# A fused attention and mixing kernel: V loaded by single transfers, first halves of keys and queries fetched first, and GpSimd bounding early weight pieces

## Chip, cores and metric

The kernel runs on one core of a Trainium2 chip. The metric is the device time of one execution in microseconds (us), lower is better. The core has a matrix engine (TensorE, PE in the rows; PEld is its weight load), VectorE (DVE), ScalarE (ACT), GpSimd (POOL), and SyncE (SP), which here only issues DMA transfers. SPq, ACTq and POOLq are the queues on which these engines issue them.

## The reference, cut to what matters

```python
def phi(x):                                   # random-feature map, 128 features
    h = einsum('bhsd,md->bhsm', x * D**-0.25, omega) - |x|^2 / 2
    return exp(h - max(h)) / sqrt(m)
q_p, k_p = phi(q), phi(k)                     # 8 batches, 8 heads, 576 rows, D = 64
kv  = einsum('bhsm,bhsd->bhmd', k_p, v);  z = sum(k_p, rows)
x   = (q_p @ kv) / (q_p @ z + 1e-6)           # [8, 576, 512] after joining the heads
u   = x + (x^T @ U @ V)^T                     # mixing over the 576 rows, rank 32
out = u + relu(u @ w_ch1) @ w_ch2             # 512 -> 2048 -> 512
```

The arrays U, V, w_ch1 and w_ch2 arrive as 64-bit floats and are turned into 32-bit floats inside the kernel.

## The kernel before

**Attention** goes over 16 units (a pair of batches by two heads each way). A round has nine steps (`for s in range(NR * NT + 7)`): round r handles the keys of one unit and the queries of an earlier one, two parts with 128 rows of 2 batches by 2 heads in each step. Round 0 handles the keys of two units. One step is a chain: the raw tile (`kt` for the first part, `qt` for the second) is transposed by VectorE, 384 columns for three steps at once (`turn`, L643); ScalarE rounds it to `xh` (L647); GpSimd takes the rest `xl` (L651); TensorE projects with `omh` and `oml` (`project`, L771 to L773) into `p_p`; VectorE takes the negated maximum `nm` (`peak`, L779); ScalarE the exponential `e` (L786); TensorE uses `e` for keys (`p_kv`) or turns it for queries (`p_q`), which ScalarE and VectorE copy to `eT` (L714) for `p_n`. Two values split one 32-bit product into three fast ones.

**Loads** of keys and queries: a raw tile has 1152 columns, of which `load(0)` brings the first 576 and `load(1)` the others, four transfers of 72 KB each (`blocks`, L616 to L626). The first group of three steps (columns 0 to 383) needs `load(0)` alone, the second (384 to 767) both. Nearly all transfers are issued by SyncE, one after the other, in an order that a list scheduler makes from the program order. The values are loaded by `load_values` (L665, L670).

**Pieces of weights** are decoded beside attention, one slot every second or third step (`decoding`, L125). The first piece is U, the next two are the halves of V (`v_jobs`, L375), then come pieces of w_ch1. For a piece, ScalarE takes the magnitude (L141) and the low word (L144), and then VectorE has three instructions: the bounds (L159, a maximum and a minimum), a shift (L160), and the sign (L163); GpSimd adds the low word (L184). `fine` is 13 in attention, the number of the pieces that are decoded this way there and just behind it. V is replicated four times over the partitions, so each half is loaded by four transfers (L381 to L385).

**Mixing** of a pair of batches (`mixing`, L418) is interleaved with the attention of the next; at the end of attention the last one overlaps with the first products of the feed-forward part. That part is done in seven-product form (`unit`, L987) with 4 column groups of w_ch1 and chunks of 512 rows, then the second matrix. The tables `BEGIN` and `PACE`, and the lists of engines in `prepare(..., lows=..., sums=...)`, are written out by hand; they say at which product a piece of helper work is emitted and on which engine it is.

## Time and profile before

| quantity | value |
|---|---|
| median of 3 runs | 1039.98 us (1036.77 to 1040.38) |
| the profiled execution's own time | 1022.2 us |
| span of the profiled execution | 1020.3 us, 23875 instructions |
| TensorE busy | 1002.5 us (98%) |
| VectorE busy | 844.5 us (83%) |
| ScalarE busy | 614.6 us (60%) |
| GpSimd busy | 516.2 us (51%) |
| mean granted TensorE clock | 0.997 of full speed |

The span runs from the first to the last instruction of the program, the execution's own time lies 1.9 us over it, and the runs without a profile are longer than both. Busy shares are means over stages with different limits: attention up to about 300 us, a transition to about 330 us, then the two matrix products of the feed-forward part.

### The profile page before, as it was taken

The page shows a single profiled execution, that of the slowest core. Times are in us where ns is not written, and L with a number is a line of the kernel's source. Part 1 is how long each engine was busy: PE and PEld are TensorE (multiplying, and loading weights), DVE is VectorE, ACT ScalarE, POOL GpSimd, SP SyncE. Part 2 cuts the span into 40 slices and gives each one's busy share as a digit, 9 for nine tenths or more (in the row PEclk, how much of TensorE's full clock was granted, in tenths as well). Part 3 has the DMA queues.
Part 4 walks back from the last instruction along what each step waited for, and adds up shares of the span by engine and source line. Part 5 has one row for each costly group of instructions (what it writes and reads, how often), then busy time and mean ns, then how long its engine had stood idle before and what let it go on. Part 6 is the DMA issues. An engine that isn't in the chain of part 4 may idle for free.

```text
span 1020.3 us, 23875 instructions
## 1 busy us (share of the span) xinstructions
PE 1002.5 (98%) x8497; PEld 980.9 (96%) x8497; DVE 844.5 (83%) x1507; ACT 614.6 (60%) x1483; POOL 516.2 (51%) x453
## 2 busy tenths in 40 slices
PE   8999999999999999999999999999999999999998
PEld 7899999999997999999999999999999999999998
DVE  4699898898899796766567565779999999999995
ACT  5889989989885557446355354665444454454442
POOL 4446966867536353323415314525756646646543
PEclk9899999999999999999999999999999999999999
DMA  7688588587444785888679768874555455455451
GB/s 141 137 164 157 115 197 161 112 188 145 88 105 113 214 202 144 225 243 207 179 204 238 183 178 273 258 234 155 176 169 204 146 176 177 145 176 176 145 177 51
DMA packets 380518, 175.51 MB, mean 172 GB/s; under 512 B 275552, under 2 KB 353376, under 8 KB 375920
## 3 DMA queue, kind: packets, MB, share of 16 engines
q1 hardware_dynamic: 378000, 173.67, 64.3%
q8 instruction: 67, 1.10, 0.5%
q10 hardware_dynamic: 2368, 0.30, 0.2%
q14 instruction: 51, 0.42, 0.1%
q0 software_dynamic: 32, 0.03, 0.0%
HBM read 109.97 MB, written 63.96 MB: 170 GB/s over the span
## 4 chain that ended last, share of the span: by engine, by line
PE 58%; DMA 1%; DVE 0%; issue 0%; ACT 0%; DVEq 0%
PE p_q L1409 10%; PE p_p L1409 10%; PE p_n L1409 7%; PE p_n L1028 7%; PE p_p L1028 5%; PE p_q L1028 5%; PE p_kv L1409 5%; PE p_kv L1028 4%; PE p_m L1028 3%; PE p_m L1409 2%; DMA raw<-in_moe_w_ch_dram 1%; DVE g L1014 0%; DMA g<-g 0%; ACT g L1010 0%; DVE u L1334 0%
## 5 line engine op out<-in xcount | busy, mean ns | idle before, releaser
L786 ACT ACTIVATE e<-p_p,nm 128x128 f32<-128x128 f32 x576 | 166.4, 397 | 24.9 <-DVE nm L779 15.9
L1247 ACT CAST gh<-gs 128x512 fp32r<-128x512 f32 x140 | 86.8, 623 | 150.4 <-DVE gs L1219 82.9
L1219 POOL TENSOR_TENSOR gs<-graw 128x512 f32<-128x512 f32 x66 | 108.5, 1654 | 125.2 <-DMA graw<-g 72.0
L1010 ACT ACTIVATE g<-g 128x512 f32<-128x512 f32 x105 | 66.4, 634 | 148.0 <-DVE g L1014 91.7
L651 POOL TENSOR_TENSOR xl<-xT,xh 128x384 fp32r<-128x384 f32 x96 | 97.5, 1033 | 99.9 <-ACT xh L647 82.8
L1254 DVE TENSOR_TENSOR gl<-gs,gh 128x512 fp32r<-128x512 f32 x140 | 132.9, 955 | 7.7 <-ACT gh L1247 6.8
L779 DVE TENSOR_REDUCE nm<-p_p 128x4 f32<-128x512 f32 x144 | 98.1, 683 | 27.4 <-ACT e L786 10.3
L184 POOL TENSOR_TENSOR wf<-wf,low 128x512 int32<-128x512 int32 (+2 forms) x35 | 44.0, 1257 | 130.0 <-ACT g L1010 71.8
L771 PE MATMUL p_p<-omh,xh 128*128 128x256 f32 x288 | 93.2, 324 | 1.9 <-ACT e L786 1.6
L1334 POOL TENSOR_TENSOR u<-u,p 128x256 f32<-128x256 f32 x72 | 80.9, 1153 | 24.8 <-DVE u L1334 22.4
L1254 DVE TENSOR_TENSOR gl<-graw,gh 128x512 fp32r<-128x512 f32 x107 | 83.1, 800 | 3.1 <-ACT gh L1247 3.1
L772 PE MATMUL p_p<-oml,xh 128*128 128x256 f32 x288 | 81.5, 283 | 0.0
L773 PE MATMUL p_p<-omh,xl 128*128 128x256 f32 x288 | 81.4, 283 | 0.0
L1409 PE MATMUL p_p<-wh,gh 128*128 128x256 f32 x288 | 79.5, 276 | 0.0
L1409 PE MATMUL p_p<-wl,gh 128*128 128x256 f32 x288 | 79.5, 276 | 0.0
L1409 PE MATMUL p_p<-wh,gl 128*128 128x256 f32 x288 | 79.5, 276 | 0.0
L1247 ACT CAST gh<-graw 128x512 fp32r<-128x512 f32 x107 | 63.7, 621 | 25.6 <-PE p_n L1409 4.9
L1409 PE MATMUL p_q<-wh,gl 128*128 128x256 f32 x276 | 76.3, 276 | 0.0
L1409 PE MATMUL p_q<-wh,gh 128*128 128x256 f32 x276 | 76.2, 276 | 0.0
L1409 PE MATMUL p_q<-wl,gh 128*128 128x256 f32 x276 | 76.2, 276 | 0.0
L729 PE MATMUL p_n<-kv,eT 128*128 128x65 f32 x512 | 73.2, 272 | 2.9 <-ACT eT L714 1.9
L729 PEld LDWEIGHTS p_n<-kv,eT 128*128 128x128 f32 x512 | 68.3, 194 | 6.2 <-ACT eT L714 2.4
(291 smaller groups left out, 3935.8 us busy)
## 6 DMA issues: line engine op xcount, KB each, us to landing
g<-g SPq DMA_DIRECT2D x282, 128.0 KB, 2.6
graw<-g SPq DMA_DIRECT2D x35, 1024.0 KB, 5.2
raw<-in_moe_w_ch_dram SPq DMA_DIRECT2D x23, 512.0 KB, 4.7
u_dram<-ut SPq DMA_DIRECT2D x36, 256.0 KB, 2.5
u<-u_dram SPq DMA_DIRECT2D x36, 256.0 KB, 2.6
out_dram<-u SPq DMA_DIRECT2D x36, 256.0 KB, 2.5
kt<-in_k_dram SPq DMA_DIRECT2D x120, 72.0 KB, 2.5
qt<-in_q_dram SPq DMA_DIRECT2D x120, 72.0 KB, 2.5
```

The source lines that it names most:

```text
L651: nc.gpsimd.tensor_tensor(out=self.xl[-1], in0=self.turned, in1=f32(self.xh[-1]), op=ALU.subtract)
L729: nc.tensor.matmul(pn[:, h, :], eT[:, h, :], kv[:, h, s // 5, :], start=True, stop=True)
L771: nc.tensor.matmul(o, part.xh[g][:, ts], oh, start=True, stop=False)
L772: nc.tensor.matmul(o, part.xh[g][:, ts], ol, start=False, stop=False)
L773: nc.tensor.matmul(o, part.xl[g][:, ts], oh, start=False, stop=True)
L779: nc.vector.tensor_reduce(out=self.nm[:, :n], in_=self.pp[:, :n], axis=AX.X, op=ALU.max, negate=True)
L786: nc.scalar.activation(out=self.e[:, j, :], in_=self.pp[:, j, :], func=AF.Exp, bias=self.nm[:, j : j + 1])
L1028: K(nc.tensor.matmul(p[:, f, :], x[:, k, fs], y[:, k, :], start=first, stop=(k == 1 and y is ul), skip_group_check=True,))
L1219: K(engine.tensor_tensor(out=to, in0=self.val[x], in1=self.val[y], op=op))
L1247: K(nc.scalar.copy(out=h, in_=v))
L1254: K(nc.vector.tensor_tensor(out=l, in0=v, in1=f32(h), op=ALU.subtract))
L1409: K(nc.tensor.matmul(acc[bank][:, half, :], x[:, ks], y[:, f, :], start=(now.s == 0 and k == 0 and half == 0 and x is h and y is wh), stop ...
```

## The change

Each half of V is loaded by one transfer with a repeated source instead of four. Omega is loaded on ScalarE's queue instead of GpSimd's, ahead of the four transfers of the second unit's first half, and the table load of ScalarE comes behind them. The halves `omh` are copied by VectorE instead of ScalarE. From the second round on, first halves are issued first: keys `load(0)`, queries `load(0)`, keys `load(1)`, queries `load(1)`, instead of both halves of the keys first. In step 3 the second part's transpose is placed behind the maximum. For pieces below 13, the bounds are applied by GpSimd right behind the magnitude, and VectorE's first slot is left empty. In the feed-forward part some helper operations change engines and some are emitted a product earlier or later.

```diff
+        bounded = fine if fine < 99 else 0
...
                 K(nc.scalar.activation(out=mags[i], in_=f32(raws[i][:, :, 1]), func=AF.Abs))
+                if i < bounded:
+                    nc.gpsimd.tensor_scalar(mags[i], mags[i], _MOST, _LEAST, ALU.min, ALU.max)
...
+            if i < bounded:
+                slots[0] = None
...
             def load(raw):
-                for j in range(4):
-                    nc.sync.dma_start(
-                        out=raw[j * R : (j + 1) * R].rearrange("r s w -> r (s w)"),
-                        in_=words(V)[:, 2 * c : 2 * c + S],
-                    )
+                rows = words(V)[:, 2 * c : 2 * c + S]
+                nc.sync.dma_start(
+                    out=raw.rearrange("p s w -> p (s w)"), in_=rows.unsqueeze(0).broadcast_to([4, R, S])
+                )
...
-                rest = nc.vector if last and t not in (0, 1, 2, 3, 4, 5, 6, 7) else nc.gpsimd
+                rest = nc.vector if last and t not in (1, 2, 3, 4, 5, 6, 7) else nc.gpsimd
...
-    nc.gpsimd.dma_start(out=once, in_=omega)
+    nc.scalar.dma_start(out=once, in_=omega)
+    keys[0].load(0)
+    keys[1].load(0, 4)
+    for p in keys:
+        p.load(1)
     nc.vector.memset(warm, 0.0)
     K(nc.scalar.activation(out=warm, in_=warm, func=AF.Exp))
-    keys[0].load(0)
-    keys[1].load(0, nc.scalar)
-    for p in keys:
-        p.load(1)
...
-        nc.scalar.copy(out=omh[r, j, :], in_=pom[r])
+        nc.vector.tensor_copy(out=omh[r, j, :], in_=pom[r])
...
                 new[0].load(0)
-                if r:
-                    new[0].load(1)
             if t == 1:
                 new.append(Queries(r + last, 1))
                 new[1].load(0)
                 if r == 0:
                     for p in keys[:2]:
                         p.load_values(1, "t")
-                    new[0].load(1)
+                new[0].load(1)
                 new[1].load(1)
...
-    BEGIN = (3, 5, 6, 9, 11, 13, 14, 16, 17, 18, 19)
+    BEGIN = (3, 5, 6, 8, 11, 13, 14, 16, 17, 18, 19)
...
-    PACE = {2: (0, 1, 1, 0, 1, 2, 1), 3: (3, 3, 3, 3, 5, 3, 0), 4: (2, 1, 2, 1, 2, 4, 2), 5: (1, 1, 2, 1, 1, 1, 2)}
+    PACE = {2: (0, 1, 1, 0, 1, 2, 1), 3: (3, 3, 4, 3, 5, 3, 0), 4: (1, 1, 2, 1, 2, 4, 2), 5: (2, 1, 1, 1, 1, 1, 2)}
```

On SyncE, these rows stand behind the load of U; they run to the values of the fourth unit's keys. `kt` and `qt` are the tiles of the third round (round 2), `x` the values of its keys. Before:

```order
L382 DMA raw<-in_moe_V_dram 32x576 x4
L665 DMA x<-in_v_dram 128x4x64 x2
L670 DMA x<-in_v_dram 64x2x64
L665 DMA x<-in_v_dram 128x4x64 x2
L670 DMA x<-in_v_dram 64x2x64
L623 DMA kt<-in_k_dram 32x18x32 x8
L623 DMA qt<-in_q_dram 32x18x32 x8
L382 DMA raw<-in_moe_V_dram 32x576 x4
L665 DMA vt_134<-in_v_dram 128x4x64 x2
```

And of the change:

```order
L387 DMA raw<-in_moe_V_dram 128x1x576
L669 DMA x<-in_v_dram 128x4x64 x2
L674 DMA x<-in_v_dram 64x2x64
L669 DMA x<-in_v_dram 128x4x64 x2
L674 DMA x<-in_v_dram 64x2x64
L627 DMA kt<-in_k_dram 32x18x32 x4
L627 DMA qt<-in_q_dram 32x18x32 x4
L627 DMA kt<-in_k_dram 32x18x32 x4
L627 DMA qt<-in_q_dram 32x18x32 x4
L387 DMA raw<-in_moe_V_dram 128x1x576
```

The first half of the queries now has seven transfers fewer ahead of it behind U: three of V and four of the keys.

On VectorE, at the first transposes of round 2 (`xT<-kt`, `xT<-qt`), with the maxima `nm` of two of the steps before it. Before:

```order
L643 STREAM_TRANSPOSE xT<-kt 128x384
L714 COPY eT<-p_q 128x256
L779 TENSOR_REDUCE nm<-p_p 128x4
L160 TENSOR_SCALAR wf<-wf 128x288
L739 TENSOR_SCALAR rec<-p_n 128x4
L643 STREAM_TRANSPOSE xT<-qt 128x384
L740 RECIPROCAL rec<-rec 128x4
```

And of the change:

```order
L647 STREAM_TRANSPOSE xT<-kt 128x384
L647 STREAM_TRANSPOSE xT<-qt 128x384
L718 COPY eT<-p_q 128x256
L783 TENSOR_REDUCE nm<-p_p 128x4
L163 TENSOR_SCALAR wf<-wf 128x288
L743 TENSOR_SCALAR rec<-p_n 128x4
```

The transpose of the queries has moved ahead of a copy `eT` and a maximum.

## Rows read from the trace of the kernel before

**Rows 1.** Busy us (x instructions) of each engine by stage: stretch, length, engines, clock, DMA.

```profile
40.00:60.00 20.00, 18.09 (x134) 17.44 (x133) 14.91 (x37) 13.53 (x47) 6.69 (x8) 0.83 0.72 131
60.00:300.00 240.00, 235.89 (x1954) 224.84 (x1952) 214.95 (x531) 215.13 (x695) 158.88 (x160) 1.00 0.69 145
100.00:120.00 20.00, 19.75 (x158) 18.57 (x156) 17.27 (x39) 19.13 (x61) 20.00 (x21) 1.00 0.75 141
300.00:330.00 30.00, 27.71 (x200) 24.31 (x199) 28.25 (x60) 19.59 (x49) 19.78 (x15) 1.00 0.52 104
330.00:480.00 150.00, 147.71 (x1254) 145.72 (x1253) 111.27 (x182) 80.98 (x156) 54.05 (x47) 1.00 0.78 205
480.00:1000.00 520.00, 519.97 (x4577) 519.70 (x4577) 443.26 (x632) 253.87 (x446) 254.31 (x184) 1.00 0.61 188
```

**Rows 2.** The same view, 38 to 52 us; order: PE, PEld, DVE, ACT, POOL, clock.

```profile
38.00:40.00 2.00, 2.00 (x20) 2.00 (x19) 0.98 (x3) 1.81 (x8) 0.92 (x1) 1.00 0.62 100
...
42.00:44.00 2.00, 0.77 (x8) 0.63 (x6) 1.86 (x7) 0.79 (x3) 0.66 (x1) 1.00 0.81 131
44.00:46.00 2.00, 1.32 (x7) 0.81 (x5) 1.96 (x5) 1.59 (x6) 1.12 (x2) 0.59 0.54 145
46.00:48.00 2.00, 2.00 (x11) 2.00 (x11) 1.29 (x4) 2.00 (x8) 0.88 (x2) 0.50 0.72 163
...
50.00:52.00 2.00, 2.00 (x15) 2.00 (x15) 0.92 (x2) 0.18 (x1) 0.00 (x0) 0.70 0.81 131
```

**Rows 3.** Timeline, 36 to 49 us, VectorE and ScalarE: start, length, instruction, [idle before].

```profile
36.93 0.57 DVE L643 STREAM_TRANSPOSE xT<-kt 128x384 f32<-128x384 f32 x1
...
38.42 0.69 DVE L779 TENSOR_REDUCE nm<-p_p 128x4 f32<-128x512 f32 x1 [0.61 <-ACT e L786]
...
42.14 0.58 DVE L643 STREAM_TRANSPOSE xT<-qt 128x384 f32<-128x384 f32 x1 [2.74 <-DMA qt<-in_q_dram]
...
43.99 1.14 ACT L786 ACTIVATE e<-p_p,nm 128x128 f32<-128x128 f32 x4 [0.46 <-DVE nm L779]
...
48.22 0.48 ACT L141 ACTIVATE wf<-raw 128x288 f32<-128x288 f32 x1
```

**Rows 4.** Timeline of SyncE's issues, 20 to 46 us: start, length, queue, transfer, count.

```profile
22.21 2.14 SPq L623 DMA_DIRECT2D qt<-in_q_dram  x4
...
26.80 1.89 SPq L382 DMA_DIRECT2D raw<-in_moe_V_dram  x4
...
32.48 5.42 SPq L623 DMA_DIRECT2D kt<-in_k_dram  x8
38.00 4.22 SPq L623 DMA_DIRECT2D qt<-in_q_dram  x8
42.75 1.78 SPq L382 DMA_DIRECT2D raw<-in_moe_V_dram  x4
```

**Rows 5.** Issue to landing of key transfers, issued 34.5 to 36.2, then 33.2 to 34.4.

```profile
DMA to landing us min/median/max: 2.3/3.5/3.9
...
DMA to landing us min/median/max: 2.3/2.5/2.5
```

**Rows 6.** Timeline, opening, and the transpose that ends round 1's second half (26.17).

```profile
1.27 0.68 POOL L809 DMA_DIRECT2D once<-in_omega_dram  x1 [0.81 <-POOLq L1460]
...
4.67 0.30 DVE L838 TENSOR_SCALAR om<-once 128x64 f32<-128x64 f32 x2 [2.65 <-DMA once<-in_omega_dram]
...
9.05 0.56 PE L771 MATMUL p_p<-omh,xh 128*128 128x256 f32 x1
...
26.17 0.58 DVE L643 STREAM_TRANSPOSE xT<-qt 128x384 f32<-128x384 f32 x1
```

**Rows 7.** GpSimd's groups up to 320 us: shapes, count, busy us, mean ns, idle before.

```profile
L184 POOL TENSOR_TENSOR wf<-wf,low 128x512 int32<-128x512 int32 x9 | 11.5, 1280 | 4.3 <-PE p_kv L683 3.0 <-DVE wf L163 1.3
...
L826 POOL MEMSET vm<- 128x260 f32 x2 | 0.6, 334 | 0.0
```

**Rows 8.** The bounds on VectorE, whole run: ns min/median/max, first and last start us.

```profile
L159 DVE TENSOR_SCALAR wf<-wf x35: 301/421/1557, 29.5 to 607.4; 128x512 f32<-128x512 f32 x32, 128x288 f32<-128x288 f32 x2, 128x320 f32<-128x320 f32 x1
```

More of the change, by code (lines that the diff above doesn't have):

```diff
@@ L276, in low @@
             h, l = (x[:, self.half, :] for x in operand(self.g, i))
-            engine = nc.vector if self.g >= EARLY_GROUPS and (0, 1, 0, 1, 0, 1, 0)[i] else self.lows
+            engine = nc.vector if self.g >= EARLY_GROUPS and (0, 1, 0, 0, 0, 1, 0)[i] else self.lows
             K(engine.tensor_tensor(out=l, in0=self.v[LEFT[i]], in1=f32(h), op=ALU.subtract))
@@ L614, in performer_mlp_kernel, with blocks @@
     ))
-    def blocks(src, raw, unit, j, queue=None):
+    def blocks(src, raw, unit, j, aside=0):
         pair, hp = unit
@@ L622, in blocks @@
                 r = h * D + a * BLK
-                (queue or nc.sync).dma_start(
+                (nc.scalar if 2 * h + a < aside else nc.sync).dma_start(
                     out=raw[r : r + BLK, j * S : (j + 1) * S].rearrange("i (b c) -> i b c", c=BLK),
@@ L634, in __init__, with load @@
             self.xh, self.xl = [], []
-        def load(self, j, queue=None):
-            blocks(self.src, self.raw, self.unit, j, queue)
+        def load(self, j, aside=0):
+            blocks(self.src, self.raw, self.unit, j, aside)
         def turn(self):
@@ L895, in performer_mlp_kernel @@
             early = prepare(
-                0, ahead, first, lows=(VE, VE, G_, G_, G_, G_, G_,), sums=(VE, G_, VE, VE,), temps=lambda: next(aside).rearrange("p (k t) -> p k t", k=2)
+                0, ahead, first, lows=(VE, VE, VE, G_, G_, G_, G_,), sums=(VE, G_, VE, VE,), temps=lambda: next(aside).rearrange("p (k t) -> p k t", k=2)
             )
@@ L912, in performer_mlp_kernel @@
                 p.copy(st.s)
-        for st in at("turn1"):
-            for p in st.group(1):
-                p.turn()
+        if s != G:
+            for st in at("turn1"):
+                for p in st.group(1):
+                    p.turn()
         for st in at("exp1"):
@@ L955, in performer_mlp_kernel @@
             st.peak()
+        if s == G:
+            for p in steps[s].group(1):
+                p.turn()
         for st in at("combine"):
@@ L1096, in performer_mlp_kernel @@
     guest_raws = loads(1, tp)
-    guest = prepare(1, next(guest_raws), place=lambda i: w_slot(NG - 1, i + 2), lows=(VE, VE, VE, VE, VE, VE, VE,), pool=tp, sums=(VE, G_, G_, G_,))
+    guest = prepare(1, next(guest_raws), place=lambda i: w_slot(NG - 1, i + 2), lows=(VE, VE, VE, VE, G_, VE, G_,), pool=tp, sums=(G_, G_, G_, G_,))
     for n, _ in enumerate(mixers[0]):
@@ L1170, in performer_mlp_kernel @@
             guest.step()
-        for _ in range((1, 1, 1, 1, 1, 1, 1)[i]):
+        for _ in range((1, 1, 1, 2, 1, 1, 1)[i]):
             chores(1, 0)
```

## The prediction

> **What bounds the kernel now.** I read the busy times by stage first. From 480 us on TensorE is busy 519.97 of 520 us, so what helper engines do there is hidden; in 330 to 480 it is idle for 150 − 147.71 = 2.29 us, in 300 to 330 for 2.29 us, and in the 240 us of attention up to 300 for 4.11 us [rows 1]. TensorE bounds nearly everything. In attention it has company: VectorE is busy 214.95 and ScalarE 215.13 of the 240 us, so a delay on either soon reaches TensorE. One early stretch stands out: 40 to 60 us, with 134 matrix products and a granted clock of 0.83, that is, partly at 1.2 instead of 2.4 GHz [rows 1].
>
> The finer table shows it. In 42 to 44 us TensorE is busy for 0.77 us only; then the granted clock is 0.59, 0.50 and later 0.70 of full speed, and 11 products fit into 2 us where 20 did before [rows 2]. The timeline says why: VectorE stands idle for 2.74 us until 42.14, waiting for the first half of round 2's queries; the maximum of the next step comes only behind that transpose, and its exponential starts at 43.99 [rows 3]. SyncE's issues say why the transfer is late: the eight transfers of keys take 5.42 us from 32.48 on, the queries start at 38.00 [rows 4]. So the place to look at is one queue, issuing without a pause in the first 45 us.
>
> **The change part by part.** The sum is made against the profiled execution, 1022.2 us (span 1020.3). The median of the runs shown is 17.8 us above it; I carry the gain over unscaled.
>
> *Opening.* Omega is issued by GpSimd at 1.27 and used at 4.67 [rows 6], 3.4 us after. A key transfer from a queue like ScalarE's takes 2.3 to 2.5 us [rows 5], and the issue need not wait for GpSimd's start, so I put the use at 3.2, 1.5 us earlier (0 to 2 as bounds), and the first projection at 7.5 instead of 9.05 [rows 6]. The price is one more issue ahead of the second keys, about 0.5 us each (8 queries in 4.22 us [rows 4]), which the same 1.5 us covers. But the gain is not kept: SyncE's order up to round 1 is unchanged. The last of its four query transfers is issued near 23.85 (22.21 and three quarters of 2.14 [rows 4]) and lands 2.3 to 2.5 us later, at 26.2, just where VectorE transposes now, at 26.17 [rows 6]. The scheduler puts one maximum ahead of that transpose, so some 1.5 us of lead survive this point, no more; what follows decides.
>
> *V by single transfers, first halves first.* Three issues of V fall away: 1.89 us become about 0.5 [rows 4], so round 2's keys start at 32.48 − 1.4 = 31.1. The eight keys hold one long issue: 5.42 − 4.22 = 1.2 us [rows 4]; four plain ones take 2.1 us. So the queries' first half is issued from 33.2 to 35.3 instead of from 38.00. Landing takes 2.3 to 2.5 us, or up to 3.9 for transfers issued shortly before the long one [rows 5]; so 37.7 to 39.2, and I take 38.2, because the long issue will fall somewhere near. That is 3.9 us before 42.14. Not all of it is gain. The transpose of the queries has moved ahead of a maximum that was done at 38.42 before [rows 3], and behind VectorE's in-order queue wait that maximum, the exponential, and then TensorE, which has projected two steps ahead and must stop. From the transpose to the next exponential it took 43.99 − 42.14 = 1.85 us [rows 3]; now that exponential is the one of the step before, so add one step. A step has at least the 1.14 us of its exponentials on ScalarE [rows 3], and about 1.6 with the copies; 38.2 + 1.85 + 1.6 = 41.65 instead of 43.99: **2.3 us** gained (1.0 to 3.3 with the landing). Late next are V's second half, now issued near 41 instead of 42.75, and round 3; ScalarE takes the former at 48.22 [rows 3], 4.2 us behind that exponential, so near 45 in the change, 4 us after its issue.
>
> *The clock.* The low stretch is about (0.41 × 2 + 0.5 × 4 + 0.3 × 2) / 0.5 = 6.8 us at half speed [rows 2] (48 to 50 taken like 46 to 48), which loses 3.4 us of work; TensorE was idle 0.68 us in 44 to 46 anyway, half of it inside that loss, so **3.1 us**. It fell behind the stop at 42 to 44. With a shorter stop I expect it to hold, 3.1 gained; if not, 0. This is the least certain term.
>
> *Bounds on GpSimd.* Thirteen instructions leave VectorE, 0.42 us each at the median and up to 1.56 [rows 8], so 5.5 us or more. GpSimd has no such instruction in the trace. Its nearest rows are a fill of 260 columns in 0.334 us, hence 0.66 for 512, and an operation on two inputs of 512 columns in 1.28 us [rows 7]; one input lies between, I take 0.9, as it is nearer to a fill in what it reads: 12 us in all (8.6 to 16.6). GpSimd is idle for 81 us of the 240 in attention [rows 1], which hides that; where it has nothing idle, in 100 to 120 [rows 1], a piece more may push an `xl` or the mixing's rest back. I count −0.5 there and +0.5 for VectorE's relief: **0** (−3 to +3). The Trainium skill's "GPSIMD Engine Reference", section 4.1 "Engine selection", says to leave elementwise work to VectorE, since GpSimd is about half as fast on two inputs and roughly at line rate on one. By its section 3.1, 512 elements take 769 ns at best, an estimate of 10 us for thirteen; the sum stays the same.
>
> *Transition and feed-forward.* One rest of the mixing goes from GpSimd to VectorE, some operand work the other way, and a few pieces move by a product. They act on 2.29 + 2.29 us of idle TensorE [rows 1]. VectorE is the fuller engine in 300 to 330 (28.25 of 30 us, GpSimd 19.78) [rows 1] and most operations leave it. I take a quarter of the idle time less what goes wrong, **0.6 us** (−1.5 to +2).
>
> Sum: 2.3 + 3.1 + 0 + 0.6 = 6.0 us; 1016.2 in a profiled execution, 1034.0 in the median.
>
> **Rivals.** *The stop stays long enough and the clock falls again.* For it: VectorE's wait only moves, from 39.4 to 42.14 before to about 36 (the keys' transpose starts at 36.93, 1.5 us earlier now) to 38.2, still 2 us, and the maximum of one step more stands behind it. Against it: transfers come earlier by 3.9 us. Then 2.3 + 0.6 = 2.9 are gained: 1037.1.
>
> *V's single transfer is the next late one.* Its four parts take 1.78 us to issue and land within some 2.5 us of the last [rows 4, 5], so 288 KB are moved in little more than 4 us. If the one transfer is spread over fewer DMA engines, say a quarter, its moving part grows from 1.78 to 7.1 us: landing at 41 + 2.5 + 7.1, 50.6 at the latest, against a use near 45. ScalarE takes it in order, with the exponentials behind it, so TensorE stops for up to 5 us (I take 3), and the clock then falls too: 6.0 − 3 − 3.1 is no gain, 1040. No row here shows a transfer with a repeated source. The Trainium skill's "DMA: Bandwidth & Descriptors", section "Why a DMA increments its semaphore by 16 and not by 1", speaks for this rival: a transfer runs on the largest number of engines up to 16 that divides the slowest dimension of both sides, which by the order's shapes would be 4 here (4 copies against 128 partitions), where the transfers of before, 32 rows on both sides, would use 16.
>
> *GpSimd becomes the bound, slower than before.* Each of the bounds that stands ahead of an `xl` on GpSimd pushes the projections of three steps back. For it: GpSimd is full in 100 to 120. If the instruction cost 1.5 us, and 12 of 19.5 us reached TensorE, the result would be 1034 + 12 = 1046; it decides from (6 + 5.2) / 13 = 0.86 us per piece that reach TensorE. Against it: the 81 idle microseconds.
>
> *VectorE's relief counts.* If a third of the 4.1 idle us up to 300 and more of the transition come back, 3 us more: 1031.
>
> **How the numbers follow.** Forecast 0.52, clock falls again 0.25, V late 0.08, GpSimd 0.08, relief 0.07. The range 1030 to 1040 takes in all but V late, GpSimd and the tails. A difference of 0.5% is 5.2 us, about what a measurement of this kernel can tell from no change. The forecast lies just beyond it: four fifths of its chance are faster, a tenth of the second rival's and all of the last: 0.51, put at 0.53. Slower is GpSimd's 0.08 with a little of V late: 0.09. The rest, 0.38, is no difference.
>
> **What would show it.** Right: the first projection near 7.5; the query transpose of round 2 near 38.2, with an idle time of about 2 us; a granted clock of 1.00 in 40 to 60; nothing lost at V's second magnitude. Wrong: a half-speed stretch within 36 to 55 us; ScalarE idle on `raw<-in_moe_V`; new waits of TensorE for `xl` or the mixing's rest; idle time in 300 to 480 above 4.6 us.

## The result and the profile after

The changed kernel takes 1034.67 us (median of 20 runs, 1030.02 to 1049.57). The kernel before takes 1027.25 us (20 runs beside them, 1019.29 to 1040.38; the three runs shown first were among its longest). The ratio is 1.0089, 95% interval 1.0068 to 1.0111, so the change costs about 9 us. Ratios here leave out disturbed runs and so can differ from the ratio of two medians; five of the profiles below (*v_four*, *before_v_single*, *v_rows*, *bounds_dve*, *bounds_alone*) are of such runs, but the 12 to 16 us that they take longer lie behind the last landmark used here. The profiled execution took 1034.45 us (span 1032.4), 12.2 us over that of before.

The stages of the changed kernel (columns as in [rows 1]: PE, PEld, DVE, ACT, POOL, clock, DMA):

```profile
20.00:40.00 20.00, 14.26 (x102) 13.55 (x100) 8.55 (x19) 13.52 (x44) 8.53 (x10) 0.84 0.68 132
...
33.00:35.00 2.00, 0.00 (x0) 0.00 (x0) 0.00 (x0) 1.21 (x3) 0.65 (x2) 0.61 0.51 101
35.00:41.00 6.00, 5.72 (x31) 5.75 (x32) 1.79 (x5) 2.53 (x9) 1.86 (x2) 0.56 0.80 130
40.00:60.00 20.00, 19.48 (x168) 18.80 (x168) 17.26 (x41) 16.30 (x56) 7.97 (x9) 0.99 0.79 128
60.00:300.00 240.00, 232.23 (x1899) 220.29 (x1897) 207.89 (x505) 208.41 (x672) 160.39 (x168) 0.99 0.68 143
...
300.00:330.00 30.00, 26.56 (x191) 23.95 (x191) 28.65 (x68) 21.56 (x64) 14.31 (x12) 0.95 0.39 78
330.00:480.00 150.00, 145.71 (x1224) 144.26 (x1224) 108.81 (x175) 78.88 (x152) 64.01 (x57) 0.99 0.77 199
480.00:1000.00 520.00, 519.43 (x4570) 518.98 (x4569) 439.83 (x627) 253.94 (x445) 249.32 (x182) 1.00 0.62 189
```

In 40 to 60 us the clock held, as forecast: 168 products at 0.99, against 134 at 0.83 [rows 1]. But 20 to 40 us has a new hole: nothing runs on TensorE from 33 to 35 us. The same stretch of the kernel before:

```profile
20.00:40.00 20.00, 19.50 (x163) 18.50 (x162) 14.29 (x30) 18.27 (x63) 8.57 (x9) 1.00 0.70 131
```

Attention to 300 us has 3.7 us more idle time, the transition 1.2 us, 330 to 480 us 2.0 us. From 480 us on it is 0.5 us. TensorE's longest waits, in 20 to 60, 60 to 300 and 300 to 480 us (total, times, longest):

```profile
PE p_kv L687 <- DMA x<-in_v_dram: 5.5, 1, 5.5
...
PE p_n L733 <- DVE eT L718: 2.1, 3, 1.5
...
PE p_kv L1034 <- DVE g L1020: 3.9, 1, 3.9
PE ph L446 <- DVE ut L454: 2.0, 1, 2.0
```

Three places, then. At the first, SyncE's issues and ScalarE say what came late:

```profile
26.73 0.78 SPq L387 DMA_DIRECT2D raw<-in_moe_V_dram  x1
27.62 0.92 SPq L669 DMA_DIRECT2D x<-in_v_dram  x2
28.64 1.18 SPq L674 DMA_DIRECT2D x<-in_v_dram  x1
29.87 2.50 SPq L669 DMA_DIRECT2D x<-in_v_dram  x2
32.42 1.84 SPq L674 DMA_DIRECT2D x<-in_v_dram  x1
34.36 2.23 SPq L627 DMA_DIRECT2D kt<-in_k_dram  x4
```
```profile
33.76 0.46 ACT L142 ACTIVATE wf<-raw 128x288 f32<-128x288 f32 x1 [2.04 <-DMA raw<-in_moe_V_dram]
...
35.28 0.66 PE L687 MATMUL p_kv<-x,e 128*128 128x65 f32 x2 [5.55 <-DMA x<-in_v_dram]
```

One issue of V is short, but V is ready 7.0 us after it, and the values `x` behind it, which TensorE wants, land late; SyncE's own next issues take longer too (2.50 and 1.84 us), and the keys of round 2 go out at 34.36, not at 32.48 [rows 4].

At the second place, near 186 us, a shift of VectorE takes 3.01 us:

```profile
185.26 0.75 POOL L283 TENSOR_TENSOR wl<-ws,wh 128x256 fp32r<-128x256 f32 x1
185.48 3.01 DVE L163 TENSOR_SCALAR wf<-wf 128x512 uint32<-128x512 uint32 x1
185.95 1.30 POOL L433 TENSOR_TENSOR ml<-x,mh 128x512 fp32r<-128x512 f32 x1
...
187.19 1.02 POOL L655 TENSOR_TENSOR xl<-xT,xh 128x384 fp32r<-128x384 f32 x1
188.42 0.57 DVE L647 STREAM_TRANSPOSE xT<-qt 128x384 f32<-128x384 f32 x1
```

It is issued while GpSimd runs `wl`, and ends only behind `ml` and `xl`. The third place, the transition and the first unit products, is taken up with the experiments.

### The profile page after: what moved, and what is told of

It reads as the page before. It is cut to its first block, busy times and chain, and to the rows that moved or that the text cites. A ratio compares the mean times of both kernels' runs of the same rounds, so it can differ in the third digit from the quotient of the medians.

```text
span 1032.4 us, 23859 instructions
## 1 busy us (share of the span) xinstructions
PE 1004.7 (97%) x8497; PEld 984.1 (95%) x8497; DVE 842.6 (82%) x1491; ACT 613.3 (59%) x1481; POOL 523.2 (51%) x470
## 4 chain that ended last, share of the span: by engine, by line
PE 55%; DVE 1%; DMA 1%; issue 1%; ACT 1%; SPq 0%; DVEq 0%; ACTq 0%
PE p_p L1415 9%; PE p_q L1415 9%; PE p_n L1415 7%; PE p_n L1034 6%; PE p_q L1034 5%; PE p_p L1034 5%; PE p_kv L1415 4%; PE p_kv L1034 3%; PE p_m L1034 3%; PE p_m L1415 2%; DVE g L1020 1%; DMA g<-g 1%; DMA graw<-g 1%; DVE wl L544 0%; DMA ts<-w_dram 0%
## 5 line engine op out<-in xcount | busy, mean ns | idle before, releaser
L790 ACT ACTIVATE e<-p_p,nm 128x128 f32<-128x128 f32 x576 | 163.7, 391 | 30.6 <-DVE nm L783 20.6
```

Source lines behind the costliest of these rows:

```text
L790: nc.scalar.activation(out=self.e[:, j, :], in_=self.pp[:, j, :], func=AF.Exp, bias=self.nm[:, j : j + 1])
```

## The experiments

Each run's trace was read at four landmarks (us from the start of the span): the start of two early maxima `nm` and of one late one, and of the 1,008th product that reads `wh` or `wl` (both counted from 0). All 144 maxima and 6,024 such products are in every trace. The last two columns before the ratio are times between landmarks: most of attention, then transition and first unit products.

| run | nm 16 | nm 32 | nm 136 | 1,008th | 32 to 136 | 136 to 1,008th | ratio to before |
|---|---|---|---|---|---|---|---|
| before | 43.23 | 76.13 | 292.36 | 446.24 | 216.23 | 153.88 | |
| changed | 46.48 | 77.57 | 299.90 | 457.96 | 222.33 | 158.06 | 1.0089 (1.0068 to 1.0111) |
| v_four | 43.88 | 74.51 | 301.81 | 461.59 | 227.30 | 159.78 | 1.0131 (1.0049 to 1.0213) |
| before_v_single | 47.23 | 78.08 | 295.73 | 448.64 | 217.65 | 152.91 | 1.0046 (0.9995 to 1.0097) |
| v_rows | 41.68 | 72.81 | 294.22 | 451.88 | 221.41 | 157.66 | 1.0072 (1.0027 to 1.0116) |
| v_other_queue | 47.57 | 78.69 | 304.60 | 461.87 | 225.91 | 157.27 | 1.011 (1.0056 to 1.0164) |
| old_tables | 46.83 | 82.51 | 302.39 | 454.33 | 219.88 | 151.94 | 1.0093 (1.0037 to 1.0148) |
| new_tables_alone | 43.56 | 74.39 | 297.19 | 454.67 | 222.80 | 157.48 | 1.0083 (1.0045 to 1.0121) |
| omega_first_halves | 42.17 | 72.32 | 296.13 | 449.08 | 223.81 | 152.95 | 0.9993 (0.9952 to 1.0033) |
| bounds_dve | 47.07 | 78.19 | 298.97 | 458.12 | 220.78 | 159.15 | 1.0089 (1.0047 to 1.013) |
| bounds_alone | 43.20 | 74.67 | 293.78 | 446.67 | 219.11 | 152.89 | 1.0023 (0.9985 to 1.0062) |
| less_v_less_tables | 42.49 | 72.99 | 306.37 | 458.95 | 233.38 | 152.58 | 1.0048 (1.0002 to 1.0094) |
| shift_two_inputs | 47.87 | 83.69 | 303.67 | 462.62 | 219.98 | 158.95 | 1.0258 (1.0194 to 1.0323) |
| less_v_two_inputs | 43.38 | 75.44 | 306.58 | 460.09 | 231.14 | 153.51 | 1.0153 (1.0088 to 1.0218) |
| gpsimd_less | 42.18 | 72.70 | 289.65 | 442.24 | 216.95 | 152.59 | 0.998 (0.9943 to 1.0018) |
| pin_shift | 42.62 | 73.32 | 296.37 | 449.34 | 223.05 | 152.97 | 1.0131 (1.0089 to 1.0174) |
| pin_before | 44.90 | 75.72 | 294.95 | 449.07 | 219.23 | 154.12 | 1.0114 (1.0073 to 1.0155) |
| pin_halves | 42.46 | 72.65 | 294.43 | 448.47 | 221.78 | 154.04 | 1.0111 (1.007 to 1.0152) |
| pin_halves_late | 42.18 | 72.62 | 289.97 | 443.93 | 217.35 | 153.96 | 0.997 (0.992 to 1.0019) |
| pin_change_late | 41.94 | 72.79 | 290.95 | 443.72 | 218.16 | 152.77 | 0.9997 (0.9952 to 1.0042) |

One profile is one execution, and two executions can differ by much. *new_tables_alone* gives every engine the same instructions in the same order as before up to 300 us, and *old_tables* the same as the changed kernel. Yet at maximum 32 the former is 1.7 us ahead of its twin and the latter 4.9 us behind, and from there to 136 they take 6.6 us more and 2.5 us less. So a difference between two traces counts below where a whole group of kernels shows it, or where the instruction that makes it can be named.

### V's single transfer

*v_four* puts four transfers back into the changed kernel, *before_v_single* puts the single one into the kernel before:

```
-    rows = words(V)[:, 2 * c : 2 * c + S]
-    nc.sync.dma_start(out=raw..., in_=rows.unsqueeze(0).broadcast_to([4, R, S]))
+    for j in range(4):
+        nc.sync.dma_start(out=raw[j * R : (j + 1) * R]..., in_=words(V)[:, 2 * c : 2 * c + S])
```

> The changed kernel with V's halves loaded by four transfers each again, all else as changed. Theory (the single transfer of V is slow and holds up the loads issued behind it): TensorE's stop of 5.5 us that ended at 35.28 us in the changed kernel goes or falls below 1.5 us, ScalarE no longer waits 2 us for V's first half, the values of the first keys land within 3.5 us of their issue instead of 5 to 8, and the granted clock stays at 1.00 there; the time is 3 to 6 us below the changed kernel's, ratio to before 1.003 to 1.006. Rival (first halves first, with its four-way interleaving of keys and queries, delays the values): the stop stays, ratio 1.008 to 1.010. A second rival, that all of the loss is in the helpers' new engines: the stop goes, but the time stays above 1.007.

> The kernel before with only V's halves loaded by one transfer each. Theory: the values behind V's first half land 5 to 8 us after issue, TensorE stops for 3 to 6 us near 35 us; ratio 1.003 to 1.006. Rival (the single transfer harms only together with first halves first): no stop above 1.5 us near 35 us and ratio 0.997 to 1.001.

The stop at 35 us follows the single transfer: 5.5 us in the changed kernel, 2.9 in *before_v_single* (3 to 6 expected), 0.9 in *v_four*. TensorE's waits for the values, of the last two:

```profile
PE p_kv L683 <- DMA x<-in_v_dram: 2.9, 1, 2.9
```
```profile
PE p_kv L687 <- DMA x<-in_v_dram: 0.9, 1, 0.9
```

At maximum 16 the single transfer alone costs 4.0 us against before, and undoing it in the changed kernel brings 2.6. The whole table agrees: of the kernels with first halves first, the five with V's repeated source reach maximum 32 at 77.57 to 83.69 us, the ten others at 72.32 to 75.44. But *v_four* lost its gain again: ScalarE's magnitude waits 3.37 us until 80.62 for a weight piece, and TensorE stops for 3.7 us. Its total is no better, 1.0131 where 1.003 to 1.006 was expected; the second rival's bound held, though its reason (all of the loss in the helpers' engines) did not.

*v_rows* tells shape from size:

```
-    in_=rows.unsqueeze(0).broadcast_to([4, R, S])          # rows = V, 32 rows
+    in_=words(w1)[:128, 2 * c : 2 * c + S]                 # 128 rows
```

> The changed kernel, with V's half taken as one transfer from 128 different rows of the first weight matrix: the same 288 KB, the same packets of 2304 bytes into the same tile, one issue, but no repeated source, so the mixing gets wrong factors. Theory by the shape (a source that repeats four times is moved by few engines): the transfer is done within 3 us of its issue, the values behind it land within 3.5 us, TensorE's stop near 35 us is below 1.5 us, and the time is 3 to 6 us below the changed kernel's, ratio 1.003 to 1.006. Rival (288 KB in one transfer hold up what is issued behind them whatever their shape): ScalarE still waits about 2 us for it, the stop stays at 4 to 6 us, ratio 1.008 to 1.010.

Issues between 24 and 34 us (number, KB each, median us to landing), of *v_rows*, and one row of the same stretch of the changed kernel:

```profile
x<-in_v_dram SPq DMA_DIRECT2D x4, 128.0 KB, 3.8
raw<-in_moe_w_ch_dram SPq DMA_DIRECT2D x1, 288.0 KB, 3.9
```
```profile
x<-in_v_dram SPq DMA_DIRECT2D x4, 128.0 KB, 7.2
```

The same bytes by one issue land in 3.9 us, where V was ready for ScalarE after 7.0, and the stop falls from 5.5 to 1.4 us. The traces' packets show why: the 128 packets of 2304 bytes take 4.9 us in the changed kernel, with at most 6 under way at once, 5.4 us with 7 in *before_v_single*, 2.3 us with 17 in *v_rows* and 2.1 us with 16 in before. So the repeated source is what makes V slow, and what is queued behind it pays. The expected ratio was missed here too (1.0072), though the 1,008th product comes 6.1 us earlier than in the changed kernel. The Trainium skill's "DMA: Bandwidth & Descriptors", section "Why a DMA increments its semaphore by 16 and not by 1", gives the repeated shape 4 engines and this one 16; the packets under way at once, 6 and 17, agree in direction.

*v_other_queue* issues the single transfers on ScalarE's queue (`nc.sync.dma_start` becomes `nc.scalar.dma_start`).

> The changed kernel with V's single transfers issued on ScalarE's queue instead of SyncE's; the first goes out in the opening, the second behind the exponentials. Theory (the single transfer is harmful because of what stands behind it on SyncE's queue and because it is used soon after its issue): the stop of 5.5 us at 35 us falls below 1.5 us, the values of the first keys land within 3.5 us, the 16th maximum at 41 to 43.5 us, and the time is 4 to 6 us below the changed kernel's. Rival (it takes the DMA engines from every queue, so it only moves the delay into the opening): the 8th maximum 1.5 us or more later than 23.31 us, the 16th at 45 us or later.

The rival was right: the stop only moves. The values land in 2.7 us now, but V goes out at 4.04 us, and in the opening SyncE's next issues take 5.89 us and VectorE waits for the first unit's keys:

```profile
4.04 1.12 ACTq L387 DMA_DIRECT2D raw<-in_moe_V_dram  x1
...
5.53 5.89 SPq L627 DMA_DIRECT2D qt<-in_k_dram  x4
...
11.63 0.58 DVE L647 STREAM_TRANSPOSE xT<-kt 128x384 f32<-128x384 f32 x1 [4.83 <-DMA kt<-in_k_dram]
```

Maximum 8 starts at 27.43 us, 4.1 us later than in the changed kernel. Here the slow transfer on another queue still delayed SyncE's. A wait of VectorE of 7.36 us at 106 us, of the kind treated below, adds to this run's time.

### The tables

*old_tables* is the changed kernel with `BEGIN`, `PACE` and the engine lists of before; *new_tables_alone* the reverse, for instance:

```
-    PACE = {2: ..., 3: (3, 3, 3, 3, 5, 3, 0), 4: (2, 1, 2, 1, 2, 4, 2), 5: (1, 1, 2, 1, 1, 1, 2)}
+    PACE = {2: ..., 3: (3, 3, 4, 3, 5, 3, 0), 4: (1, 1, 2, 1, 2, 4, 2), 5: (2, 1, 1, 1, 1, 1, 2)}
```

> The changed kernel with the hand-written tables and engine lists of the transition and of the feed-forward part as before, attention untouched. Theory (the retuned tables cost in the feed-forward part what attention does not explain): TensorE's stops of 2.0 us at 324 us and 3.9 us at 382 us fall below 1.0 us each, the stop at 35 us (5.5 us) and the one at 190 us (1.5 us) stay, and the 1,008th weight product starts 3 to 5 us earlier than the changed kernel's 457.96 us, so between 453 and 455 us; the time is about 4 us below the changed kernel's. Rival (both stops follow from attention, which hands over its last rests late): they stay at 2 and 3 to 5 us, the 1,008th product at 457 to 459 us.

> The kernel before with only the new tables and engine lists of the transition and the feed-forward part. Theory (these tables cost by themselves): stops of 1.5 to 2.5 us at 315 to 320 us and 3 to 5 us at 370 to 378 us, the 1,008th weight product 3 to 5 us behind the 446.24 us of the kernel before; ratio 1.002 to 1.005. Rival (they harm only behind the changed attention): the product at 445 to 447.5 us, ratio 0.998 to 1.002.

This is the clearest part. From maximum 136 to the 1,008th product all seven kernels with the new tables take 157.3 to 159.8 us, all thirteen with the old ones 151.9 to 154.1. TensorE's longest waits in 300 to 480 us, of *new_tables_alone*, then of *old_tables*:

```profile
PE p_kv L1028 <- DVE g L1014: 3.4, 2, 3.1
PE ph L442 <- DVE ut L450: 2.0, 1, 2.0
```
```profile
PE p_kv L1034 <- DVE g L1020: 1.1, 2, 0.9
PE p_q L713 <- ACT eT L718: 0.9, 2, 0.6
```

Near 322 us in the changed kernel two of VectorE's sums stretch from 0.68 to 1.65 us beside GpSimd's `ml` (in *old_tables* one), and `ut` comes late:

```profile
319.89 1.28 POOL L433 TENSOR_TENSOR ml<-x,mh 128x512 fp32r<-128x512 f32 x1
320.07 1.65 DVE L535 TENSOR_TENSOR x<-x 128x512 f32<-128x512 f32 x1
...
321.71 1.27 POOL L433 TENSOR_TENSOR ml<-x,mh 128x512 fp32r<-128x512 f32 x1 [0.55 <-ACT mh L431]
...
321.90 1.64 DVE L535 TENSOR_TENSOR x<-x 128x512 f32<-128x512 f32 x1
```

Which entry of the tables does it was not separated. The expectations of the place held, but the 1,008th product of *new_tables_alone* comes 8.4 us after that of before, not 3 to 5, and both ratios lie above theirs. The totals do not add up from such parts: the tables alone cost 1.0083, more than their 3.6 us behind maximum 136, and the change without them 1.0093, no less than with them. In the trace of *old_tables* V's second half stops ScalarE too, 1.51 us at 53.07, 8.3 us after its issue at 44.72, and maximum 32 is 4.9 us later than in the changed kernel, with the same instructions up to there.

### First halves first, and where its lead goes

*omega_first_halves* keeps only the opening, the order of the halves and the moved turn.

> The kernel before with only omega first on ScalarE's queue, first halves first and the turn behind the maximum in the third step; V by four transfers, bounds on VectorE, old tables. Theory (this part of the change is the gain that was forecast, the others are the loss): no stop of TensorE above 1.5 us up to 60 us, the 16th maximum 1.5 to 3 us earlier than 43.23 us and still 1.5 to 3 us ahead at maximum 80 (175.05 us before); ratio 0.996 to 0.999. Rival (the lead is used up by new stops that the new order makes anywhere in attention): at maximum 136 no lead against 292.36 us, ratio 0.999 to 1.004.

It is 3.8 us ahead at maximum 32, with a clock of 1.00 in 40 to 60 us. Then ScalarE meets a weight piece that SyncE issued at 72.56, against 71.67 in before, in spite of the lead:

```profile
77.44 0.66 ACT L141 ACTIVATE wf<-raw 128x512 f32<-128x512 f32 x1 [2.38 <-DMA raw<-in_moe_w_ch_dram]
```

TensorE stops for 2.8 us there and for 3.1 us at 123 us, behind a wait of VectorE of 5.08 us; by maximum 136 it is 3.8 us behind. The rival was right. (*new_tables_alone*, in the order of before, was 1.7 us ahead at maximum 32 and lost it to the same two stops, of 1.7 and 3.1 us.)

### VectorE behind GpSimd

*bounds_dve* and *bounds_alone* undo and do the bounds on GpSimd alone (`bounded = 0`; the two lines of the diff put into the kernel before).

> The changed kernel with the bounds of the early pieces on VectorE again. Theory (GpSimd's added instructions lengthen VectorE's waits in the decoding, above all the 3.0 us of a shift at 185 us): no shift above 1.3 us in attention, no half-speed stretch near 190 us, the lag against the kernel before does not grow between 180 and 200 us; the time is 2 to 5 us below the changed kernel's, ratio 1.004 to 1.007. Rival (the bounds on GpSimd cost nothing, as predicted, and the stop at 189 us is a chance of the order): ratio 1.007 to 1.011, the lag at 200 us stays near 7 us. The stop near 35 us stays at 5 to 6 us in either.

> The kernel before with only the bounds of the early pieces on GpSimd. Theory (neutral, as forecast: VectorE loses thirteen instructions of about 0.6 us, but the shifts wait longer behind GpSimd): no bounds on VectorE near 118 us, so no wait of 5.1 us there; a shift of 1.9 to 3.1 us somewhere in attention; GpSimd takes 0.61 us for each of the bounds; the 1,008th weight product between 445 and 449 us (446.24 before), ratio 0.997 to 1.002. Rival (the bounds on GpSimd are a loss of their own): from maximum 32 to 136 it takes 4 us or more longer than the 216.2 us of before, ratio 1.004 or more.

In *bounds_dve* the 3.0 us at 186 us went, but VectorE's bounds waited 5.09 us at 120 (and the stop near 35 us was 3.7 us, not 5 to 6). *bounds_alone* is level with before (446.67 against 446.24; ratio 1.0023, 0.9985 to 1.0062). In sum the bounds are neutral; the long waits come with either, at different places. From maximum 80 to 88 the eight kernels with bounds on VectorE take 17.5 to 17.6 us and the twelve with bounds on GpSimd 18.0 to 22.6, the changed kernel the most. From 48 to 56 three of the eight take 22.8 to 23.7 us, all with bounds that last 5.1 us, and all other kernels 17.4 to 19.5. *less_v_less_tables* combines everything in the change but V and the tables:

> The changed kernel without the single transfers of V and without the new tables and engine lists: omega first, first halves first, the turn behind the maximum and the bounds on GpSimd remain. Theory (these two parts are the whole loss): no stop of TensorE above 1.6 us up to 60 us, from maximum 136 to the 1,008th weight product 152 to 154 us (158.1 in the changed kernel), the product at 444 to 449 us, ratio 0.996 to 1.000. Rival (what remains of the change costs by itself in attention): the product at 451 us or later, ratio above 1.003.

It was not faster, and its trace beside that of *bounds_alone* shows why. The same shift, with the same instructions of GpSimd around it; first *bounds_alone*, then *less_v_less_tables*:

```profile
102.30 0.75 POOL L278 TENSOR_TENSOR wl<-ws,wh 128x256 fp32r<-128x256 f32 x1
102.38 0.97 DVE L160 TENSOR_SCALAR wf<-wf 128x512 uint32<-128x512 uint32 x1
103.00 1.48 POOL L429 TENSOR_TENSOR ml<-x,mh 128x512 fp32r<-128x512 f32 x1
```
```profile
105.02 0.76 POOL L278 TENSOR_TENSOR wl<-ws,wh 128x256 fp32r<-128x256 f32 x1
105.12 7.35 DVE L160 TENSOR_SCALAR wf<-wf 128x512 uint32<-128x512 uint32 x1
105.71 1.31 POOL L429 TENSOR_TENSOR ml<-x,mh 128x512 fp32r<-128x512 f32 x1
106.95 1.98 POOL L651 TENSOR_TENSOR xl<-xT,xh 128x384 fp32r<-128x384 f32 x2
...
111.44 0.75 POOL L278 TENSOR_TENSOR wl<-wf,wh 128x256 fp32r<-128x256 f32 x1
```

In both the shift is issued 0.1 us into `wl`. In one it gets in when `wl` ends; in the other GpSimd goes on with seven more instructions without a gap, and the shift ends just behind the last. The same happened to the same instructions in two executions; first before, then *new_tables_alone*:

```profile
118.00 1.24 DVE L159 TENSOR_SCALAR wf<-wf 128x512 f32<-128x512 f32 x1
```
```profile
117.66 5.08 DVE L159 TENSOR_SCALAR wf<-wf 128x512 f32<-128x512 f32 x1
```

So a part of what attention takes in an execution is which side such a meeting falls on. The Trainium skill's "SBUF — State Buffer", section "Who interferes with whom", says that VectorE and GpSimd share a port pair and that, where an instruction of VectorE uses both of its ports, as `tensor_scalar` can, whichever issues first holds the pair for its whole instruction; the waits agree, their length over several instructions is more than that section says.

*shift_two_inputs* (and *less_v_two_inputs*, early pieces alone) gives the shift a second tensor input:

```
-    nc.vector.tensor_scalar(words(m), words(m), 3, 0x3FFFFFFF, ...)
+    nc.vector.scalar_tensor_tensor(words(m), words(m), 3, low30.broadcast_to([P, n]), ...)
```

> The changed kernel with VectorE's shift of each decoded piece written as an instruction with two tensor inputs (the mask is read from a tile of one column, repeated), the same result. Theory (the one-input shift waits until GpSimd leaves off altogether, one with two inputs for one instruction of GpSimd at most): the instruction takes 0.6 to 0.8 us at the median instead of 0.32, but none in attention takes over 1.7 us where one took 3.0; TensorE's stop at 190 us goes, and the lag against the kernel before grows by under 2 us from maximum 80 to 88 instead of by 4.9. Rival (VectorE waits for GpSimd's run whatever the form): an instruction of 2.5 us or more remains. The stop at 35 us stays in either.

> The run before this one, with VectorE's shift of the early pieces as an instruction with two tensor inputs. Theory (the one-input form is what waits through several instructions of GpSimd): no decoding instruction of VectorE above 1.7 us in attention, from maximum 32 to 136 in 215 to 219 us, ratio 0.994 to 0.999, the fastest of all. Rival (twice the time of the instruction costs what the shorter wait gives): 220 us or more between these maxima, ratio 0.999 to 1.003.

In the first nothing exceeded 1.52 us in attention. In the second this form took 7.64 us at 103.65, through eight instructions of GpSimd. My theory that the form decides has fallen; that the first has no long wait shows also that one trace without it proves little.

*gpsimd_less* takes `ml` away from *less_v_less_tables* (outside the last mixing); the pin runs add a wait to GpSimd's order, behind the shift (*pin_shift*) or behind bounds and shift (*pin_before*, *pin_halves*):

```
     tc.keep_in_program_order(slot())
+    ...                       # for the pieces and instructions named
+    nc.gpsimd.tensor_scalar(pin, m[:, :1], _MOST, _LEAST, ALU.min, ALU.max)
```

> The run less_v_less_tables with the rests of the mixing's input left out in all mixings but the last (the rounded values stand in their place, so the result is less exact), which takes 1.3 us per part from GpSimd. Theory (unbroken runs of GpSimd make the long waits): GpSimd's longest run without a gap near 105 us shrinks, no decoding instruction of VectorE above 2 us in attention, no stop of TensorE above 2 us between 85 and 230 us. Rival (the long waits have another cause): one above 3 us remains.

> The run less_v_less_tables with one more small instruction on GpSimd behind each of VectorE's shifts of early pieces: it reads one column of the shift's result, so GpSimd must let the shift through before it goes on. Theory (VectorE does not get its turn as long as GpSimd has the next instruction ready): no shift in attention above 1.7 us (7.35 there), TensorE's stop of 5.3 us near 113 us is gone, GpSimd stands idle for at most 1.5 us ahead of each added instruction; the 1,008th weight product at 447 to 451 us, ratio 0.998 to 1.001, and the scatter of the times is smaller. Rival (the long duration is not due to GpSimd's order): a shift above 3 us remains.

> The kernel before with the same small instruction on GpSimd behind the bounds and behind the shift of each early piece. Theory: the bounds near 118 us, which took 1.24 us in the profile of before and 5.08 us in two later runs, take under 1.7 us always; the times scatter less, the median falls by 0 to 3 us, ratio 0.997 to 1.001. Rival (GpSimd's added waits delay its rests and with them the projections): ratio 1.001 to 1.006, TensorE waits for xl.

> The run omega_first_halves with the small instruction behind bounds and shift. Theory: the wait of 5.08 us at 117 us and TensorE's stop of 3.1 us behind it are gone, the 1,008th weight product at 445 to 447.5 us instead of 449.1, ratio 0.995 to 0.999, so that this is the fastest. Rival (GpSimd's waits cost the same elsewhere): the product at 449 us or later, ratio 0.999 or more.

Without `ml` no decoding instruction in attention takes over 1.50 us, no stop is above 1.5 us, and maximum 136 comes 16.7 us earlier than in *less_v_less_tables*. With the pins the longest in attention is 1.39 us (*pin_shift*) or 2.37 (the other two), and the times lie within 4.5, 2.7 and 3.3 us. That GpSimd's unbroken runs make the long waits is seen in each of them: the instruction ends just behind such a run. That a pin prevents them is likely from these traces, not proven. The totals disappointed (1.011 to 1.013) for another reason: these three kernels, like the two with `low30`, hold one more tile of one column, and TensorE is slower in the whole feed-forward part. 700 to 1000 us of *pin_halves*, then of *pin_halves_late*, whose pin is written into a tile that was there:

```profile
700.00:1000.00 300.00, 300.00 (x2601) 300.00 (x2600) 287.39 (x394) 135.09 (x235) 172.69 (x128) 1.00 0.49 164
```
```profile
700.00:1000.00 300.00, 300.00 (x2650) 300.00 (x2648) 291.06 (x402) 136.35 (x238) 174.92 (x129) 1.00 0.50 166
```

The two last runs also load second halves a step later (from the second round on), so that the weight piece goes ahead of them:

```
-                new[0].load(1)
-                new[1].load(1)
+            if t == 2 and r:
+                new[0].load(1)
+                new[1].load(1)
```

> The run pin_halves with two edits: the result of the added instruction goes into an existing tile, and from the second round on the second halves of keys and queries are loaded a step later, so that a weight piece's load stands ahead of them on SyncE. Theory: 336 weight products take 38.1 us again behind the 2,016th (38.8 in pin_halves), so the slower rate came from the one more tile, which moves the tiles behind it; TensorE's stop of 3.7 us at 80 us falls below 1 us, maximum 136 at 290.5 to 292.5 us instead of 294.4, the time 12 to 15 us below pin_halves, ratio 0.993 to 0.998 with little scatter. Rivals: the rate stays at 38.8 (the added instructions themselves slow it, ratio 1.007 or more); or the second halves now come late, with a stop of 1.5 us or more at another place between 50 and 100 us.

> The same two edits on pin_shift: all of the change in attention but V's single transfers (omega first, first halves first, bounds on GpSimd), tables as before, the added instruction behind the shifts, second halves a step later. Theory: 38.1 us for 336 products, no stop above 1 us between 50 and 300 us, maximum 136 at 291 to 293.5 us instead of 296.4, ratio 0.994 to 0.999. If bounds on GpSimd are a gain at all, maximum 136 comes earlier here than in pin_halves_late; rival: it comes 1 us or more later, since GpSimd's work is on the path.

In the traces both do what was expected or nearly: no stop at 80 us, 16.4 and 15.4 us at maximum 136 ahead of *less_v_less_tables*, 2.3 and 2.5 us ahead of before at the 1,008th product. The medians are 1022.85 and 1022.77 us, beside 1028.32 us of before in the same runs, the ratios 0.997 (0.992 to 1.002) and 0.9997 (0.995 to 1.004): not slower, and no proven gain (0.994 to 0.999 was expected of the second). The scatter did not shrink here, against my expectation: 1018.8 to 1034.5 and 1019.7 to 1036.4 us. So the meetings of the two engines are not what makes the largest part of it; that stays open. Maximum 136 comes 1.0 us later with the bounds on GpSimd, the 1,008th product 0.2 us earlier: neutral once more.

## Why the prediction was wrong

The forecast time, 1034.0 us, lies next to the measured 1034.67 by accident: it was worked out from a median of 1039.98 us that more runs put at 1027.25. What was claimed, 6 us of gain, was a loss of 9.

*Opening, 1.5 us, not kept:* right. The first projection starts at 6.66 us (7.5 forecast, 9.05 before), the first maximum starts at 10.00 instead of 12.21 us, maximum 8 at 23.31 instead of 24.95.

*V by single transfers, first halves first, 2.3 us:* the step that failed is "three issues of V fall away: 1.89 us become about 0.5". It priced the issue and not the transfer. The rival that did, V late by being spread over a quarter of the engines, was there, but with 0.08 and at the second half alone, where a slack of 4 us seemed to lie ahead of its use. The first half is used sooner, and the values behind it sooner still. Measured, the transfer's packets took 4.9 us, the half was ready 7.0 us after its issue, and TensorE stood idle for 5.55 us. That sets the start of the loss: 1.6 us ahead at maximum 8, 3.3 us behind at 16. With V by four transfers a lead was there: at maximum 32 *omega_first_halves* is 3.8 us ahead of before, and 2.1 to 3.4 us ahead of *new_tables_alone*, *bounds_alone* and *pin_before*, which keep the old order of loads; 2.3 were forecast without the clock.

*The clock, 3.1 us:* in 40 to 60 us it held (0.99), but the largest term of the sum stood on one execution. The three kernels just named keep the order of loads of before, and their clock in 40 to 60 us is 1.00, with 155, 151 and 153 products. In *bounds_alone* VectorE's wait and TensorE's stop are those of before [rows 2, 3], and no fall follows:

```profile
42.10 0.58 DVE L643 STREAM_TRANSPOSE xT<-qt 128x384 f32<-128x384 f32 x1 [2.74 <-DMA qt<-in_q_dram]
```
```profile
42.00:44.00 2.00, 0.75 (x7) 0.62 (x6) 1.90 (x7) 0.83 (x3) 0.69 (x1) 1.00 0.77 123
...
46.00:48.00 2.00, 2.00 (x20) 2.00 (x20) 1.93 (x7) 2.00 (x8) 0.93 (x2) 1.00 0.70 159
```

So in three of the four profiled executions with this order of loads there was no fall to win back, and most of the 3.1 us was not there to be won. A fall came with the new stops instead: the granted clock was 0.61 and then 0.56 of full speed in 33 to 35 and 35 to 41 us, so part of it at 1.2 GHz, while and after TensorE stood idle for 5.55 us. The rival had the right mechanism in the wrong place.

*Bounds on GpSimd, 0:* right as a sum (1.0023), and cheaper than the 0.9 us assumed: 0.61 us each at the median. But the wait behind GpSimd was not priced at all. VectorE's twelve shifts in attention go from a median of 0.60 to 0.97 us, up to 3.01, and from 7.8 to 12.2 us in sum, which eats more than half of the 7.6 us that the bounds had taken there.

*Transition and feed-forward, 0.6 us (−1.5 to +2):* wrong in sign and bound. The step was "they act on 2.29 + 2.29 us of idle TensorE": moving helpers can also make idle time, and did, 4.2 us between maximum 136 and the 1,008th product, 3.6 in *new_tables_alone*.

By landmarks the profiled lag of 11.7 us at the 1,008th product is 1.4 us up to maximum 32 (the lead of first halves less V), 6.1 us from there to 136, and 4.2 us behind it. Up to 32 the cause is shown, though not its size in every execution, and for the last part that it is the tables. Of the 6.1 us in the middle 5.0 lie between maxima 80 and 88, where the shift waits 3.01 us behind GpSimd and TensorE stops for 1.5 us; with the bounds back on VectorE (*bounds_dve*) this stretch takes 17.6 us again, as in before. But *bounds_dve* then loses more than 4 us from 48 to 56, at the wait that the profiled execution of before escaped and *new_tables_alone*, with the same instructions, did not. So how much of the middle part is a loss in the mean of many executions stays open.

## What to carry to other kernels

Price a merged transfer by its landing and by what is queued behind it, not by the issues it saves; a source repeated in its slowest dimension made 288 KB take 7.0 us instead of 3.9. A fall of the clock that one profile shows is worth a term of the sum only if a second execution has it too: here the largest term was not of that kind. A lead won early lasts only to the next transfer that is issued in a fixed order: move that one too, or the gain is handed back. Tables that were tuned for one order of work are part of it, so run them apart from the change that they came with, and where totals scatter by more than the effect compare kernels at landmarks, in more than one trace each.

## What was not expected of the hardware

VectorE can wait through a whole unbroken run of GpSimd: 7.35 us in the one-input and 7.64 us in the two-input form, where the one-input shift took 0.97 us elsewhere.

With a single tile of 128 x 1 values more TensorE's products were 1.9% slower at a granted clock of 1.00 (2650 / 2601 in 300 us), in all five kernels that had it; 336 products took 38.8 us instead of 38.1. That the tile does it by moving the tiles behind it is a guess; which operand's place matters was not tried.
